# Batch 1 of a Fourier mixing kernel in the form of batches 2 to 7, its additions at written-out times, the extra channel two steps later, and two chunks' last row through TensorE

## The chip, the cores and the metric

The kernel runs on one core of one Trainium2 chip. The metric is the device time of one execution in microseconds (us); the time before is the median of three runs. Engine names in the profile: PE (TensorE, the matrix engine; PEld is its weight loads), DVE (VectorE), ACT (ScalarE), POOL (GpSimd), SP (SyncE, which here only issues DMAs).

## The reference

The input `x` has 8 batches of 3008 rows and 256 channels. Each batch goes through a two-dimensional Fourier transform (over rows and over channels), of which the real part is kept. The result, as 24064 rows of 256, goes through a two-layer network with an ELU between:

```python
X = np.fft.fft(np.fft.fft(x, axis=1), axis=2).real
h = X.reshape(24064, 256) @ w_in                    # w_in: 256 x 2048
g = np.where(h > 0, h, np.exp(np.minimum(h, 0)) - 1)
out = g @ w_out                                     # w_out: 2048 x 256
```

`x` is float32; `w_in` and `w_out` come as 64-bit floats and are converted on the chip.

## The kernel before, in words

**Use of symmetry.** The real part of the transform is a cosine part minus a sine part. Rows k and 3008 - k of the result share both parts with opposite signs, so the kernel computes 1504 columns per batch (one per row pair), 12032 in all, and gets two output rows from each. The channel transform is folded into the first weight matrix: `Wsc` holds the cosine half `Wc` and the sine half `Ws` of the folded `w_in`.

**The main loop.** The columns are cut into 47 tiles of 256, and the 16 blocks of 128 hidden units into 8 pairs. One pair of one tile is a slot; there are 376, some 4.75 us each. A slot does: P, two matmuls of `Wc` with the ring buffer `Rr` into a PSUM bank H (`mm_P`); V, VectorE adding the one extra channel with the weights `wex` (`even_part`, line 1352, writes E); Q, two matmuls of `Ws` with the ring `Ir` into the same bank (`mm_Q`); the minus row from E and H (line 1366); the ELU of both rows (four ACT instructions, two VectorE instructions at line 1382, all into G); four sums on POOL (`sum_1` to `sum_4`); and seven matmuls with `w_out` (`mm_X1` to `mm_X3`, from slot 16 on; eight plain ones, `mm_plain`, before). H has three PSUM banks.

**The transforms.** The rings hold 2048 columns, so a batch's transform must be done shortly before its columns come up: batch 1 begins in tile 5 (slot 40). For each batch there are four: cosine or sine (`ri`) by even or odd output index (`kodd`). Each is made of an even and an odd half, one PSUM bank each, placed between two slots. Two forms exist:

- `Dft` (batches 0 and 1): rows s, 1504 - s and their mirrors are folded first (`mirror_folds` for batch 1, thirty POOL instructions on tiles of 128 x 1536), then three matmuls per half: widths 189, 189 and 378 for the even half and three of 377 for the odd half (or 188, 188, 376 and three of 376). The matrices are `MC`.
- `Quarter` (batches 2 to 7): the rows are folded once more. A batch is loaded in a near and a far set of 96 (or 94) partitions and four rows each (`load_quarter` by indirect DMA on POOL or by SP, `load_odd` by SP), then come `mirror_sum` (POOL), `half_sum` (VectorE), `channel_fold` (POOL), `channel_edge` (ACT), `quarter_pairs` (POOL for even, VectorE for odd index), `turn_pairs` and `shift_pairs` (VectorE). Each half then takes four matmuls, of about 95 columns each (or, for the odd index's odd half, 95 and 94). The matrices are `QM`, 96 rows of them. `unfold`, `finish`, `unfold_odd` and `join` on VectorE put the result into the rings.

**The weights.** `w_in` and `w_out` come in eight chunks each. `Chunk.steps` converts one: exponent and mantissa by integer instructions on VectorE (lines 408 and 420), three ACT steps, then on POOL a rounding sum (line 603, "w<-raw,w"), on VectorE the sign (line 462), on POOL the product and, for `w_in`, two pair sums. The tiles named pow are shared: the next chunk's exponent step waits for the product before. Chunks 5 to 7 of `w_in` and 4 to 7 of `w_out` are converted in slots 7 to 14. `fold_chunk` folds a chunk of `w_in` by TensorE, `put_chunk` copies it to `Wsc` on ACT. The last row of `Ws` must also become two columns of `wex`: for chunks 0 and 1 by `turn_last_row` (two one-column matmuls) and `put_last_row` (ACT), for chunks 2 to 7 by `spread_last_row`, two SP DMAs through DRAM.

**The extra channel.** Channel 128 of all batches is loaded separately (`load_ext`, `get_ext`), folded, transformed by twelve matmuls (`dft_ext`), copied to SBUF (`ext_side`), unfolded and added on VectorE into the tile `rx`, and from DRAM spread over the ring `Rb` (`spread_ext`).

**The order.** Every piece of work is an event with a nominal time: `at(t, fn)`, with 4.8 us per slot (T). The list `FRONT` gives the first 34 us by name, the rest is slot times T plus an offset. Events are sorted and emitted, and `pin` keeps this order on each compute engine; an engine runs its instructions strictly in that order. DMAs issued on SP without `pin` may be placed elsewhere by the scheduler of the framework; on SP too, each waits for the one ahead. Nominal times only order the work; real times are later (slot 12 has nominal 57.6 us and its P begins at 97.55).

Of the kernel before, what the change touches and what calls it, by code (L numbers as in the profile page):

```python
# [9 lines left out]
FP = mybir.dt.float32  # L10
# [167 lines left out]
def kernel(  # L178
# [381 lines left out]
    def load_quarter_mats(ri, kodd):  # L560
        t = cpool.tile([128, BW], FP, tag=f"MC{ri}{kodd}", name=f"QM{ri}{kodd}")
        QM[ri, kodd] = t
        n = sum(QW[i % 2] for i in range(2 * ri + kodd))
        nc.sync.dma_start(
            out=t[0:96, 0 : QW[kodd]], in_=QM_dr.ap()[:, n : n + QW[kodd]]
        )
# [166 lines left out]
    def mirror_folds(L):  # L733

        ops = []
        rows = [t.rearrange("p (m d) -> p m d", d=ND) for t in L]
        for j, k in ((3, 2), (0, 1)):
            own, other = rows[j], rows[k][:, ::-1]
            for m in range(6):
                ops.append(  # L740
                    lambda own=own, other=other, m=m: gtt(
                        own[:, m, 1:], own[:, m, 1:], other[:, m, :0:-1], ALU.add
                    )
                )
            ops.append(
                lambda own=own, other=other: gtt(
                    own[:, :, 0:1], own[:, :, 0:1], other[:, :, 0:1], ALU.add
                )
            )
        EO = [None] * 4  # L750
        for kodd in range(2):
            z = L[1 + kodd]
            for n in range(4):
                c = slice(384 * n, 384 * n + 384)
                ops.append(
                    lambda z=z, c=c, kodd=kodd: gtt(
                        z[:, c], L[0][:, c], L[3][:, c],
                        ALU.subtract if kodd else ALU.add,
                    )
                )  # L760
            for ri in range(2):
                t = EO[2 * ri + kodd] = spool.tile(
                    [128, 768], FP, tag=f"{'eo'[ri]}{1 + 2 * kodd}", bufs=1, name="eo"
                )
                for h in range(2):

                    def fold(z=rows[1 + kodd], t=t, ri=ri, h=h):
                        src = z[:, 3 * h : 3 * h + 3]
                        lo, hi = (
                            v.rearrange("p m (d o) -> p m o d", o=2)  # L770
                            for v in (src[:, :, 1:129], src[:, :, 255:127:-1])
                        )
                        o = t[:, 384 * h : 384 * h + 384]
                        o = o.rearrange("p (m o d) -> p m o d", o=2, d=64)
                        if ri:
                            gtt(o, lo, hi, ALU.subtract)
                        else:
                            gtt(o, lo[:, :, ::-1], hi[:, :, ::-1], ALU.add)

                    ops.append(fold)  # L780
                if not ri:
                    o = t.rearrange("p (m o d) -> p m o d", o=2, d=64)
                    state["edge", kodd] = lambda o=o, z=rows[1 + kodd]: act(
                        o[:, :, 0, 63:64], z[:, :, 0:1]
                    )
        return EO, ops

    def lines(j, far):

        return state["L", j, far].rearrange("p (m d) -> p m d", d=ND)  # L790

    def mirror_sum(j, far, m):

# [6 lines left out]
    def half_sum(kodd, far, h):  # L800
# [3 lines left out]
        for m in (2 * h, 2 * h + 1):  # L804
            vtt(o[:, 3 - m], a[:, m], b[:, m], ALU.subtract if kodd else ALU.add)
# [1321 lines left out]
```

## Time and profile before

| | |
|---|---|
| median of three runs | 1906.9 us (1906.72 to 1908.05) |
| the profiled execution | 1907.61 us |
| its span, first to last instruction | 1905.8 us |
| granted TensorE clock | 1.000 |
| TensorE busy | 1896.7 us |
| VectorE busy | 1488.2 us |
| POOL busy | 1353.5 us |
| ACT busy | 880.2 us |

A line of the timeline gives start, length, engine, line of the kernel, operation, the tiles it writes and reads, how many such instructions follow each other, and in brackets the idle time before it with what ended that. A TensorE matmul in float32 is recorded as two records (so "x4" is two matmuls). Their ends are modelled, so a small gap on PE is better read from the starts: records of 256 columns follow each other every 0.216 us. A line of the groups gives count, total busy time in us, mean in ns, and idle time in front with its releasers.

### The profile page before, as it was taken

The numbers are of one execution on the slowest core, as the hardware profiler recorded it, in microseconds if no ns is written. First come the engines' busy times: TensorE is split into PE (matmuls) and PEld (weight loads), VectorE is DVE, ScalarE is ACT, GpSimd is POOL, SyncE is SP. The second block draws the span as 40 slices with busy tenths as digits, with TensorE's granted clock in tenths as the row PEclk, the third lists the DMA queues.
The fourth block names the chain that finished last, engine by engine and source line by source line (L and its number), as shares of the span: only waits on it lengthen the run. The fifth ranks groups of instructions, "written<-read, shape, count | busy, mean of one in ns | idle before, by whom it ended". The sixth has DMA issues, their size and how long they took to land.

```text
span 1905.8 us, 27983 instructions
## 1 busy us (share of the span) xinstructions
PE 1896.7 (100%) x8972; PEld 1646.7 (86%) x8972; DVE 1488.2 (78%) x2836; ACT 880.2 (46%) x1723; POOL 1353.5 (71%) x1846
## 2 busy tenths in 40 slices
PE   9999999999999999999999999999999999999999
PEld 6888888888888888888888888888888888888887
DVE  8766667888878888778877788877888778777666
ACT  5754444444444444444444444444444444444443
POOL 4887667786677766777667777687766777556664
PEclk9999999999999999999999999999999999999999
DMA  8146211211011110111102111022110210100101
GB/s 340 45 33 44 54 24 45 53 24 36 12 45 41 32 33 12 46 40 30 31 20 49 35 27 30 13 56 44 25 24 16 55 20 15 17 12 15 20 12 23
DMA packets 278934, 73.66 MB, mean 39 GB/s; under 512 B 254402, under 2 KB 268998, under 8 KB 278788
## 3 DMA queue, kind: packets, MB, share of 16 engines
q1 hardware_dynamic: 270148, 61.44, 16.0%
q0 software_dynamic: 6464, 10.18, 1.7%
q8 instruction: 71, 1.16, 0.3%
q14 instruction: 75, 0.61, 0.1%
q10 hardware_dynamic: 2176, 0.26, 0.1%
HBM read 46.96 MB, written 24.80 MB: 38 GB/s over the span
## 4 chain that ended last, share of the span: by engine, by line
PE 96%; DVE 2%; DMA 1%; ACT 1%; issue 0%; POOL 0%; ACTq 0%; POOLq 0%; DVEq 0%
PE H L594 37%; PE pB L594 17%; PE pC L594 17%; PE pD L594 17%; PE pA L594 9%; DMA xl<-in_x_dram,ix 0%; DVE e L691 0%; DVE E L1352 0%; DVE o L691 0%; DVE pow L462 0%; POOL w L603 0%; ACT Wsc L606 0%; ACT G L606 0%; ACT M L606 0%; DMA wex<-wx 0%
## 5 line engine op out<-in xcount | busy, mean ns | idle before, releaser
L603 POOL TENSOR_TENSOR G<-G 128x256 f32<-128x256 f32 x1437 | 1047.4, 738 | 498.6 <-DVE G L1382 343.6
L606 ACT ACTIVATE G<-H 128x512 f32<-128x512 f32 x376 | 224.8, 598 | 917.4 <-DVE G L1366 913.7
L1352 DVE SCALAR_TENSOR_TENSOR E<-Rb,wex,H 128x256 f32<-128x256 f32 x752 | 327.7, 477 | 310.8 <-PE H L594 303.9
L594 PE MATMUL H<-Rr,Wsc 128*128 128x256 f32 x1504 | 388.0, 380 | 0.5 <-ACT Wsc L606 0.5
L594 PE MATMUL H<-Ir,Wsc 128*128 128x256 f32 x1504 | 386.8, 380 | 1.5 <-DVE E L1352 1.5
L594 PE MATMUL pC<-G,WT 128*128 128x256 f32 x1440 | 369.5, 379 | 0.0
L594 PEld LDWEIGHTS H<-Ir,Wsc 128*128 128x128 f32 x1504 | 278.5, 189 | 49.3 <-DVE E L1352 3.9
L594 PEld LDWEIGHTS H<-Rr,Wsc 128*128 128x128 f32 x1504 | 281.6, 190 | 41.6 <-issue 2.3
L594 PEld LDWEIGHTS pC<-G,WT 128*128 128x128 f32 x1440 | 273.6, 190 | 37.2
L1366 DVE SCALAR_TENSOR_TENSOR G<-E,H 128x512 f32<-128x512 f32 x376 | 257.4, 685 | 45.1 <-POOL G L603 11.8
L1382 DVE SCALAR_TENSOR_TENSOR G<-G,H 128x512 f32<-128x512 f32 x376 | 256.4, 682 | 40.0 <-ACT G L606 39.9
L1382 DVE SCALAR_TENSOR_TENSOR G<-M,G 128x512 f32<-128x512 f32 x376 | 257.5, 685 | 0.7 <-ACT M L606 0.7
L606 ACT ACTIVATE G<-G 128x512 f32<-128x512 f32 x376 | 233.4, 621 | 0.0
L594 PE MATMUL pA<-G,w 128*128 128x256 f32 x784 | 229.4, 379 | 0.0
L594 PE MATMUL pB<-G,w 128*128 128x256 f32 x784 | 229.3, 379 | 0.0
L594 PE MATMUL pD<-G,w 128*128 128x256 f32 x784 | 229.3, 379 | 0.0
L606 ACT ACTIVATE M<-G 128x512 f32<-128x512 f32 x376 | 224.1, 596 | 2.8 <-DVE G L1366 1.5
L606 ACT ACTIVATE M<-M 128x512 f32<-128x512 f32 x376 | 221.1, 588 | 0.1
L594 PE MATMUL pB<-G,WT 128*128 128x256 f32 x720 | 214.6, 380 | 0.0
L594 PE MATMUL pD<-G,WT 128*128 128x256 f32 x720 | 214.2, 379 | 0.0
L594 PEld LDWEIGHTS pA<-G,w 128*128 128x128 f32 x784 | 148.9, 190 | 20.7 <-DVE G L1382 0.3
L594 PEld LDWEIGHTS pB<-G,w 128*128 128x128 f32 x784 | 148.9, 190 | 20.4 <-PE H L594 0.2
(171 smaller groups left out, 1584.2 us busy)
## 6 DMA issues: line engine op xcount, KB each, us to landing
out_dram<-ot SPq DMA_DIRECT2D x496, 32.0 KB
xq<-in_x_dram SPq DMA_DIRECT2D x48, 94.0 KB
out_dram<-ot SPq DMA_DIRECT2D x256, 2.0 KB
Rb<-r SPq DMA_DIRECT2D x10, 376.0 KB
raw<-in_moe_w_in_dram SPq DMA_DIRECT2D x7, 512.0 KB
MC<-dft_mats SPq DMA_DIRECT2D x3, 943.5 KB
xq<-in_x_dram SPq DMA_DIRECT2D x12, 192.0 KB
xq<-in_x_dram SPq DMA_DIRECT2D x36, 64.0 KB
```

What stands on the lines that cost most here:

```text
L594: nc.tensor.matmul(out_, lhsT=lhsT, rhs=rhs, start=start, stop=stop, skip_group_check=True)
L603: pin(nc.gpsimd.tensor_tensor(out=o, in0=a, in1=b, op=op))
L606: pin(nc.scalar.activation(out=o, in_=i, func=func, **kw))
L1352: nc.vector.scalar_tensor_tensor(out=S.E[:, c], in0=Rb[:, cols(i)], scalar=wex[:, f : f + 1], in1=S.H[:, c], op0=ALU.mult, op1=ALU.add,)
L1366: nc.vector.scalar_tensor_tensor(out=two(S.G[:, 0:512])[:, :, ::-1], in0=two(S.E), scalar=2.0, in1=two(S.H), op0=ALU.mult, op1=ALU.subtract,)
L1382: nc.vector.scalar_tensor_tensor(out=o, in0=e, scalar=-1.0, in1=h, op0=ALU.add, op1=ALU.max)
```

## The change

Batch 1 is loaded, folded and transformed in the `Quarter` form; `mirror_folds`, `load_x` for batch 1, and the helpers `at_half` and `at_dft` go. In `FRONT`, the four near loads of batch 1 stand at 14.06 (lines 3 and 0 from SP), 15.24 and 16.44 (line 2), 16.44 and 19.2 (line 1); its far loads come at 56.3 to 71.5. All its folding steps stand at times of their own. The four transforms begin at steps 28, 34, 38 and 44 (before: 26, 34, 37, 42).

The four quarter matrices share the two sine `MC` tiles (`MC10`, `MC11`) and are loaded at 34.6 nominal in place of 245 to 288; the turn table moves from step 34 to step 8, the index table (`quarter_table`, four small POOL instructions) from step 27 to 10.0. The extra channel's loads move by 0.8 steps, its transform from step 29 to 31; the copies `ext_side` now stand together in step 32 (before: two in step 30, two in step 33), the odd index's copies lie in free parts of `rx`, and `ext_unfold`, `ext_up` and `ext_down` of the even index stand together in step 32 (before: steps 30, 31 and 32). Chunks 6 and 7 of `w_in` get their last row by `turn_last_row` and `put_last_row`.

```diff
-    def load_quarter_mats(ri, kodd):
-        t = cpool.tile([128, BW], FP, tag=f"MC{ri}{kodd}", name=f"QM{ri}{kodd}")
...
+        home = [
+            cpool.tile([128, BW], FP, tag=f"MC1{i}", name=f"QM{i}") for i in range(2)
+        ]
+        for ri in range(2):
+            for kodd in range(2):
+                w = QW[kodd]
+                c = 0 if ri else QW[1 - kodd]
+                QM[ri, kodd] = t = home[ri == kodd][:, c : c + w]
+                nc.sync.dma_start(out=t[0:96], in_=QM_dr.ap()[:, n : n + w])
+                n += w
...
-    def mirror_folds(L):
...
-    def half_sum(kodd, far, h):
+    def half_sum(kodd, far, h, tt):
...
-            vtt(o[:, 3 - m], a[:, m], b[:, m], ALU.subtract if kodd else ALU.add)
+            tt(o[:, 3 - m], a[:, m], b[:, m], ALU.subtract if kodd else ALU.add)
...
-        t = spool.tile([128, 384], FP, tag="side", bufs=2, name="side")
+        if kodd and rows == NB:
+            t = state["rx"][:, RUN + NO * (1 - par) :]
+        else:
+            t = spool.tile([128, 384], FP, tag="side", bufs=2, name="side")
...
-    names["L"] = lambda: [open_x(1)] + [state["loads"][n]() for n in (4, 5)]
-    for n in range(4):
-        names[f"L{n}"] = lambda n=n: state["loads"][n]()
+    names["L"] = lambda: [
+        fn(1, j, 0) for j in (3, 0) for fn in (load_quarter, load_odd)
+    ]
+    for n, (fn, j) in enumerate(
+        ((load_quarter, 2), (load_odd, 2), (load_quarter, 1), (load_odd, 1))
+    ):
+        names[f"L{n}"] = lambda fn=fn, j=j: fn(1, j, 0)
...
-        (16.44, "w3p u3b Wc2 Xb1 b+3 w3R h3"),
+        (16.44, "w3p u3b Wc2 Xb1 b+3 w3R h3 L1 L2"),
...
-    for c, t in ((2, 15.2435), (3, 23.1265)) + tuple((c, (2 * c - 1) * T + 0.04) for c in range(4, 8)):
+    for c, t in ((2, 15.2435), (3, 23.1265)) + tuple((c, (2 * c - 1) * T + 0.04) for c in (4, 5)):
         at(t, lambda c=c: spread_last_row(c))
+    for c in (6, 7):
+        at((2 * c - 1) * T + 3.02, lambda c=c: turn_last_row(c))
+        at((2 * c - 1) * T + 3.03, lambda c=c: put_last_row(c))
...
-    at(29 * T + 4.75, dft_ext)
-    at(30 * T + 1.46, lambda: ext_side(0))
-    at(30 * T + 1.47, lambda: ext_side(1))
-    at(30 * T + 4.25, lambda: ext_unfold(0, vtt))
-    at(31 * T + 4.25, ext_up)
-    at(32 * T + 4.25, ext_down)
-    at(33 * T + 1.46, lambda: ext_side(2))
-    at(33 * T + 1.47, lambda: ext_side(3))
...
+    at(31 * T + 4.75, dft_ext)
+    at(32 * T + 1.46, lambda: ext_side(0))
+    at(32 * T + 1.47, lambda: ext_side(1))
+    at(32 * T + 1.48, ext_open)
+    for g in (2, 3):
+        at(32 * T + 1.49, lambda g=g: ext_side(g))
+    at(10.0, quarter_table)
+    at(7.2 * T, load_quarter_mats)
...
-    for step, ri, kodd in ((26, 0, 0), (34, 1, 0), (37, 0, 1), (42, 1, 1)):
-        at_dft(step, 2, 1, ri, kodd, lambda k=2 * ri + kodd: state["EO"][k])
...
+    for t, fn, *key in (
+        (23.22, mirror_sum, 3, 0, 1),
+        (26.00, quarter_row, 1),
+        (28.00, mirror_sum, 3, 0, 0),
+        (29.07, mirror_sum, 3, 0, 3),
+        (30.13, mirror_sum, 0, 0, 2),
+        (32.31, mirror_sum, 0, 0, 1),
+        (33.05, mirror_sum, 0, 0, 3),
+        (33.06, mirror_sum, 0, 0, 0),
+        (39.32, mirror_sum, 3, 0, 2),
+        (39.33, half_sum, 1, 0, 0, vtt),
+        (44.10, half_sum, 0, 0, 0, vtt),
+        (44.12, half_sum, 0, 0, 1, vtt),
+        (44.52, channel_fold, 0, 0, 0, 0),
+        (44.52, half_sum, 1, 0, 1, vtt),
+        (45.23, channel_fold, 1, 0, 0, 0),
+        (46.73, channel_fold, 0, 1, 0, 0),
+        (51.51, channel_fold, 1, 0, 0, 1),
+        (52.26, channel_fold, 0, 0, 0, 1),
+        (55.43, channel_edge, 0, 0),
+        (56.33, load_quarter, 1, 0, 1),
+        (56.38, load_odd, 1, 0, 1),
+        (58.91, channel_fold, 1, 1, 0, 0),
...
+        (61.86, channel_fold, 0, 1, 0, 1),
+        (63.71, load_quarter, 1, 3, 1),
...
+        (68.12, channel_fold, 1, 1, 0, 1),
...
+        (76.02, mirror_sum, 0, 1, 0),
...
+        (155.20, ext_unfold, 0, vtt),
+        (156.21, ext_up, 0, vtt),
+        (157.11, ext_down, 0, vtt),
...
+    ):
+        at(t, lambda fn=fn, key=key: fn(*key))
+
+    for step, ri, kodd, finish, join in ((28, 0, 0, 0, 31), (34, 1, 0, 0, 37), (38, 0, 1, 42, 53), (44, 1, 1, 50, 54)):
+        at_quarter(step, 1, ri, kodd, finish, join)
```

## The prediction

> **What bounds the kernel now.** First I read the page's busy times and its chain of work that ended last: is one engine the bound from end to end?
>
> ```profile
> PE 1896.7 (100%) x8972; PEld 1646.7 (86%) x8972; DVE 1488.2 (78%) x2836; ACT 880.2 (46%) x1723; POOL 1353.5 (71%) x1846
> ...
> PE 96%; DVE 2%; DMA 1%; ACT 1%; issue 0%; POOL 0%; ACTq 0%; POOLq 0%; DVEq 0%
> ```
>
> TensorE is on the chain for 96% of the span, so a matmul removed shortens the run unless a new wait appears. The chain in order of time gives the prices. Columns are start, length, what; "PE H x10" is four ordinary H records (0.86) and the six of one half transform of batch 1, "x12" is four and the eight of one half transform of batch 2.
>
> ```profile
> 157.25 0.86 PE H L594 x4
> ...
> 173.22 2.14 PE H L594 x10
> ...
> 184.86 2.77 PE H L594 x10
> ...
> 431.91 1.76 PE H L594 x12
> ```
>
> Third, the waits of PE and its timeline (start, length, idle before it). Records issue every 0.216 us, so eight take 1.73 and a gap is read from start to start. Five gaps behind 30 us matter here: 34.65 (0.77), 59.62 (0.70), 101.02 (98.41 + 1.73 = 100.14, so 0.88), 112.95 (110.62 + 1.73, so 0.60) and 215.36 (0.3).
>
> ```profile
> 59.62 1.13 PE L594 MATMUL H<-Rr,Wsc 128*128 128x256 f32 x4 [0.54 <-ACT Wsc L606]
> ...
> 101.02 1.13 PE L594 MATMUL H<-Ir,Wsc 128*128 128x256 f32 x4 [0.72 <-DVE E L1352]
> ...
> 112.95 1.13 PE L594 MATMUL H<-Ir,Wsc 128*128 128x256 f32 x4 [0.44 <-DVE E L1352]
> ```
> ```profile
> 215.36 1.13 PE L594 MATMUL H<-Ir,Wsc 128*128 128x256 f32 x4 [0.31 <-DVE E L1352]
> ```
>
> VectorE's timeline says what made E late: at 98.88 a chunk's exponent step waited for POOL's product (the shared tile pow), at 112.03 the extra row's weights were still in a DMA.
>
> ```profile
> 98.88 0.43 DVE L408 TENSOR_SCALAR pow<-raw 128x512 int32<-128x512 int32 x1 [2.17 <-POOL w L603]
> ...
> 102.08 2.30 DVE L462 SCALAR_TENSOR_TENSOR pow<-raw,pow 128x512 int32<-128x512 int32 x1
> ...
> 112.03 0.87 DVE L1352 SCALAR_TENSOR_TENSOR E<-Rb,wex,H 128x256 f32<-128x256 f32 x2 [1.92 <-DMA wex<-wx]
> ```
>
> **The change, part by part.** The sum is made on the profiled execution (1907.61 us, span 1905.8) and taken as a difference from the median, 1906.9, which is 0.7 below it.
>
> *Transforms of batch 1 on TensorE.* Eight half transforms go. Their chain pieces are 2.14, 2.77, 2.14, 2.77, 2.13, 2.76, 2.13, 2.76 = 19.60; less 8 x 0.86 of ordinary H work this is 12.72 us. Batch 2's eight pieces are all 1.76: 8 x (1.76 - 0.86) = 7.20. On the path, since PE has no cover: **-5.52 us**. Ends: 7.20 is a like-for-like row, so I give it 0.1 either way. In those pieces a 95-column record takes 0.112 us; a 256-column one, at 0.216, would scale to 0.080. [...]
>
> *Last row of chunks 6 and 7.* Two SP DMAs each go; two one-column matmuls (four records) and a small copy on ACT come. The only clear row is the same step for chunk 1: it starts at 34.65 and the next matmul at 35.12, so 0.47 each: **+0.94**. Chunk 7's DMA was what released E at 112.03, so its 0.60 gap goes: **-0.60**. Chunk 6's DMAs were issued at 94.31 and 95.47 and E of its slot began at 100.10, behind VectorE; nothing is won. The new wait: PE now stands behind ACT's copy of the folded chunk to Wsc. For chunk 6 that copy ends at 94.29 and PE reaches the place at 95.82: covered by 1.5. For chunk 7 it ends at 108.25 and PE arrives at 108.03; queued behind are all later matmuls. Price 0 if the 2.30 us exponent step at 102.08 shortens, 1.0 if that chain slips with the slot 12 delay below; I take **+0.2**, the measured difference.
>
> *The first sums, slots 5 to 14.* POOL had 14 mirror instructions in slots 6 to 9 (twelve of mean 0.94 us) and almost no idle from 71.3 to 94.9. Now seven mirror sums (0.73, in the later batches' rows) stand before slot 7, where POOL was idle 3.56 us, one in slot 8, three folds (0.84 each) in slot 9 and two in slot 10. Its four near indirect DMAs become two, with two more in slots 11.7 and 13.3 (1.2 each); SP's four large loads become sixteen of 0.4 us, in a stretch where SP stands idle till 41.48. VectorE gets the half sums: 2 instructions behind E of slot 8, 6 behind E of slot 9. Nearest row:
>
> ```profile
> L600 DVE TENSOR_TENSOR xq<-xq,xq 96x256 f32<-96x256 f32 x48 | 32.7, 718 | 0.0
> ```
>
> A 256-wide addition with one PSUM operand takes 0.415 (u<-v,pC). Cover: VectorE's idle before E, 1.30 us in slot 8 and 2.89 in slot 9. Two at 0.72 are 1.44, so E of slot 9 moves from 80.02 to about 80.2, still before its matmul at 81.54. Six at 0.42 are 2.5 and fit into 2.89; six at 0.72 are 4.3 and would move E of slot 10 by 1.4, past its margin of 0.66 (start 87.39, latest 88.05): a stall of 0.8. In that stretch POOL waits for ACT until about 84, so I take the lower: 0. [...]
>
> Does the 0.88 gap at 101.02 go? POOL's backlog does, but the chain into it is serial: the minus step of slot 10 ended at 91.0, nine ACT steps ran to 96.12, then two POOL steps of 1.3, then the exponent steps. ACT, later by the half sums, starts that chain at about 91.4. Ends: -0.88 and +0.8; I take **+0.2**.
>
> *Far loads, the weight sums, slots 12 to 17.* POOL gains two DMAs (2.4) and two folds (1.7) against one half sum of 1.0 before the conversion at 112.87, in front of which it sat idle 3.05: covered. Behind it, a fold and a mirror sum (1.6) replace two half sums (2.0) before the first tile sums at 130.16. **0.**
>
> *Slots 17 to 56.* Per batch, VectorE's groups of the later batches add up to some 43 us (half sums 11, turns 15, the rest 17) against 7 for the old form: +36 in 46 slots that have about 1.85 idle each, 85 in all. POOL: 30 against 29. A tile sum may come about 1.5 us late (sum 2 ended at 155.1, its matmul at 156.66). Crowded is slot 32: four side copies on ACT (0.48 each, two before), then three additions for the extra channel (1.22 for the pair, 0.67, 0.61; formerly one slot each): 2.5 us into 1.85, less what waits for ACT anyway. Ends 0 and 0.9; I take **+0.2**. Taking the other two side copies out of slot 33 removes the late G behind the 215.36 gap: **-0.3**. The quarter matrices and turn table load 120 us earlier than needed: 0; the iotas are 0.46 on POOL ahead of a 1.3 us margin: 0.
>
> Sum: -5.52 + 0.94 - 0.60 + 0.2 + 0.2 + 0.2 - 0.3 = **-4.9**: 1906.9 - 4.9 = **1902.0 us** (the profiled execution by itself: 1902.7).
>
> **Rivals.**
> - *The backlog was the cause.* With POOL free the exponent step waits no more: the 0.88 gap, the 0.2 at slot 12 and the 0.2 wait for the chunk copy go. For it: POOL without idle for 23 us. Against it: the serial ACT chain. 1902.0 - 1.3 = 1900.7.
> - *Collisions in the first sums.* Half sums at 0.72, E of slot 10 late (0.8), the copy of chunk 7 late (1.0 in place of 0.2), slot 32 at its upper end (0.9 in place of 0.2). For it: the conversion steps at 0.95 and 1.51 beside 0.42. 1902.0 + 2.3 = 1904.3: within 0.2%.
> - *Slower: batch 1's lines come late.* The first mirror sum now stands in POOL's queue at about 52.5 us, before two weight chunks; POOL waits in order. Slack is the 1.24 idle at 56.42; after that every microsecond of lateness passes to the copy at 58.98 and the matmul at 59.62. It decides from 1.24 + 4.9 = 6.1 us late, and is slower by over 0.2% from 9.9; at 10 late 1910.8. For it: SP's queue is in order, and the wx issue sat until 43.64. Against it: VectorE's last read of those tiles started at 16.9 us, and the loads of before were out by 34.7.
>
> That the form doesn't change is excluded: all four of batch 1's transforms go to the quarter class.
>
> **How the numbers follow.** 0.2% is about what a measurement of this kernel can tell from no change: 3.8 us, so faster means under 1903.1. The likeliest case has 0.58, its own range is 1901.2 to 1903.3 (slot 12, the copy and slot 32 at their nearer ends), and all but 0.06 of it is faster. The backlog rival has 0.14, the collisions 0.19, late lines 0.09. Faster: 0.52 + 0.14 = 0.66; same: 0.06 + 0.19 = 0.25; slower: 0.09. The range runs from 1900.6 (the backlog rival) to 1905.4 (the collision rival, and 1.1 for a slot 12 gap that doubles beside it); outside it lie the late lines and a little of the rest.
>
> **What would show it.** In the chain, batch 1's pieces read about 1.76 with x12 and no x10 is left beyond 170 us. One-column matmuls stand 0.47 apart twice more, and no E waits for wex from 105 on. The PE gap near 101 is still 0.7 to 1.2, near 215 none. VectorE's half sums of slot 9 read about 0.42 each; at 0.7 the collisions hold, and E of slot 10 starts after 88. POOL's first mirror sum starts by 53 with no DMA as its releaser. The prediction is wrong if PE gaps between 50 and 250 us add up to more than 4, or if the 95-column records stand wider than 0.112.

## The result, and the profile after

The changed kernel takes 1912.32 us (median of 8 runs, 1910.78 to 1917.63) where the kernel before takes 1906.9 us (8 runs, 1906.69 to 1908.05): 1.0030 times as long, with a 95% interval of 1.0021 to 1.0039. It is slower by about 5.4 us; the forecast was 1902.0 and faster. Its times also spread wider than before's. The profiled execution is one of the two long ones, 1917.45 us with a span of 1915.7, so the account below is of such a run. One execution each of two later versions, e12 and e13, took 2630 and 2478 us at a granted clock of 0.71 and 0.75; the times below leave them out.

The page of the changed kernel: busy times, and the chain that ended last.

```profile
PE 1895.8 (99%) x8996; PEld 1647.7 (86%) x8996; DVE 1518.6 (79%) x2910; ACT 880.8 (46%) x1731; POOL 1357.7 (71%) x1858
...
PE 88%; DMA 2%; SPq 1%; DVE 1%; POOL 0%; issue 0%; ACTq 0%; ACT 0%; DVEq 0%; POOLq 0%
```

TensorE's share of the chain fell from 96% to 88%, and SP's queue is on the chain for the first time. The work itself became shorter, as forecast; in the chain in order of time the five pieces of batch 1 that stand on it read like batch 2's (two of them here), and the other three take the same 0.86 us from start to start in the timeline:

```profile
230.13 1.76 PE H L600 x12
253.09 1.76 PE H L600 x12
```

What was lost are waits. TensorE's timeline of the changed kernel (start, length, idle before it and what ended that):

```profile
52.73 1.13 PE L600 MATMUL H<-Ir,Wsc 128*128 128x256 f32 x4 [2.62 <-DVE E L1292]
...
92.46 1.13 PE L600 MATMUL H<-Ir,Wsc 128*128 128x256 f32 x4 [0.81 <-DVE E L1292]
...
99.49 1.13 PE L600 MATMUL H<-Ir,Wsc 128*128 128x256 f32 x4 [0.72 <-DVE E L1292]
...
106.56 1.13 PE L600 MATMUL H<-Ir,Wsc 128*128 128x256 f32 x4 [1.17 <-DVE E L1292]
...
208.75 2.07 PE L600 MATMUL H<-Ir,Wsc 128*128 128x256 f32 x4 [6.31 <-DVE E L1292]
...
244.56 0.70 PE L600 MATMUL pB<-G,WT 128*128 128x256 f32 x2 [0.55 <-POOL G L609]
```

Read from start to start, as the prediction did, each gap is some 0.16 longer, and the record behind it starts another 0.10 late (the four records from 52.73 on take 0.97 us, to 53.70, and not 0.86). A gap of 0.73 at 62.20 is the one that the kernel before has at 59.62. The others fall into three places.

**A, 52.73 us.** VectorE's E of the third chunk's slot stood for 2.66 us waiting for the extra row's weights:

```profile
51.80 0.87 DVE L1292 SCALAR_TENSOR_TENSOR E<-Rb,wex,H 128x256 f32<-128x256 f32 x2 [2.66 <-DMA wex<-wx]
```

SP's issue of that DMA in this trace, and in the kernel before with the E that needed it:

```profile
45.83 0.52 SPq L652 DMA_DIRECT2D wex<-wx  x1
```
```profile
45.94 0.39 SPq L646 DMA_DIRECT2D wex<-wx  x1
48.76 0.88 DVE L1352 SCALAR_TENSOR_TENSOR E<-Rb,wex,H 128x256 f32<-128x256 f32 x2 [0.43 <-PE H L594]
```

It was not late but slow: it landed after some 5.9 us, where before it was there by 48.76, in 2.8 at most. Ahead of it in SP's queue now stand batch 1's near loads, ten of them from 31.43 to 40.12 and three more between the two DMAs of the extra row. From its issue to its landing the DMA engines were busy for 0.27 of the time (before: 0.05), so they were not full; how the loads in front would slow it, these traces do not show.

**C, 92 to 107 us.** VectorE's timeline: its half sums in slot 9, and the conversion steps behind them.

```profile
83.75 2.09 DVE L606 TENSOR_TENSOR xq<-xq,xq 96x256 f32<-96x256 f32 x6
...
88.87 1.34 DVE L408 TENSOR_SCALAR pow<-raw 128x512 int32<-128x512 int32 x1
90.14 1.49 DVE L420 TENSOR_SCALAR w<-raw 128x512 int32<-128x512 int32 x1
91.55 0.86 DVE L1292 SCALAR_TENSOR_TENSOR E<-Rb,wex,H 128x256 f32<-128x256 f32 x2
...
93.53 2.44 DVE L462 SCALAR_TENSOR_TENSOR pow<-raw,pow 128x512 int32<-128x512 int32 x1
```

The same places of the slots in the kernel before:

```profile
83.21 0.42 DVE L408 TENSOR_SCALAR pow<-raw 128x512 int32<-128x512 int32 x1
83.55 0.95 DVE L420 TENSOR_SCALAR w<-raw 128x512 int32<-128x512 int32 x1
87.39 0.87 DVE L1352 SCALAR_TENSOR_TENSOR E<-Rb,wex,H 128x256 f32<-128x256 f32 x2 [2.89 <-PE H L594]
...
89.38 1.04 DVE L462 SCALAR_TENSOR_TENSOR pow<-raw,pow 128x512 int32<-128x512 int32 x1
```

The six half sums of slot 9 cost 0.35 us each and the two of slot 8 0.60, both less than forecast. The steps behind them cost more: 1.34, 1.49 and 2.44 us where 0.42, 0.95 and 1.04 stood. E of slot 10 starts at 91.55 with no idle time before it, so TensorE waits for it. The third gap, at 106.56, is the one that the forecast knew at 101.02 (an exponent step that waits for POOL's product); it grew by 0.45.

**D, 200 to 250 us.** ScalarE's and VectorE's timelines around 207 us:

```profile
206.63 0.42 ACT L612 ACTIVATE xq<-xq 1x256 f32<-1x256 f32 x1 [9.85 <-DMA xq<-in_x_dram]
206.96 0.19 ACT L612 ACTIVATE o<-xq 94x4 f32<-94x4 f32 x1
```
```profile
207.18 0.73 DVE L832 SCALAR_TENSOR_TENSOR o<-o,twist_tab,e 94x128 f32<-94x128 f32 x2 [8.70 <-ACT o L612]
```

ScalarE's one-row copy for batch 2 (quarter_row) waited 9.85 us for batch 2's near lines; behind it in ScalarE's order stood batch 1's channel edge, behind that a turn on VectorE, behind that E, behind that TensorE. SP's queue says why these lines were late; first the changed kernel, then the kernel before:

```profile
127.54 2.65 SPq L319 DMA_DIRECT2D xq<-in_x_dram  x6
130.28 8.30 SPq L1133 DMA_DIRECT2D x<-in_x_dram  x4
...
188.12 10.71 SPq L1133 DMA_DIRECT2D x<-in_x_dram  x4
198.92 2.64 SPq L319 DMA_DIRECT2D xq<-in_x_dram  x1
```
```profile
109.81 6.20 SPq L1182 DMA_DIRECT2D x<-in_x_dram  x4
...
164.34 6.67 SPq L1182 DMA_DIRECT2D x<-in_x_dram  x4
```

The extra channel's 16 loads (load_ext: 1,536 single elements each) began 20.5 us later than before, of which some 5 are the delay of everything behind A and C. Batch 1's far loads of line 2 stand ahead of them, and in front of those SP waited 7.6 us for the landing of the second of POOL's far gathers (the changed kernel, POOL's timeline and SP's waits from 112 to 130 us: how much in total, how often, the longest):

```profile
115.55 1.53 POOL L303 DMA_INDIRECT xq<-in_x_dram,ix  x1 [0.18 <-issue]
```
```profile
SPq L336 <- DMA xq<-in_x_dram,ix: 12.3, 2, 7.6
```

That gather landed at 126.78, 11.2 us after its start, and SP's next load went out at 126.79. A POOL fold that the same loads also need, among the weight sums at 122.44, had ended by 123.3. Their last four ended at 198.8 instead of 171.0, and batch 2's first near load followed at 198.92. The consumers had been moved by two slots, some 10 us; the loads moved by 20 to 28.

**The account of this execution**, every gap read from start to start. Transforms -5.5; one-column matmuls of chunks 6 and 7 +0.7, and +0.2 since the record behind each pair is 0.08 late; the two gaps that went, -0.6 and -0.5; A +2.8; C: three gaps of 0.97, 0.88 and 1.33 against one of 0.88, +2.3; D: 6.5 at 208.75, 1.9 for the slow records behind it (last section) and 1.9 in four small waits for POOL, +10.3; the second late record behind each gap, seven against three, +0.4; a front that ended 0.3 earlier, -0.3. Together +9.8; measured, span against span, +9.9.

### The profile page after: what moved, and what is told of

Same layout as the page of the kernel before. It is cut to its first block, busy times and chain, and to the rows that moved or that the text cites. A ratio compares the mean times of both kernels' runs of the same rounds, so it can differ in the third digit from the quotient of the medians.

```text
span 1915.7 us, 28156 instructions
## 1 busy us (share of the span) xinstructions
PE 1895.8 (99%) x8996; PEld 1647.7 (86%) x8996; DVE 1518.6 (79%) x2910; ACT 880.8 (46%) x1731; POOL 1357.7 (71%) x1858
## 3 DMA queue, kind: packets, MB, share of 16 engines
q1 hardware_dynamic: 271638, 62.20, 16.5%
## 4 chain that ended last, share of the span: by engine, by line
PE 88%; DMA 2%; SPq 1%; DVE 1%; POOL 0%; issue 0%; ACTq 0%; ACT 0%; DVEq 0%; POOLq 0%
PE H L600 34%; PE pB L600 16%; PE pC L600 15%; PE pD L600 15%; PE pA L600 8%; DMA x<-in_x_dram 1%; SPq L1527 0%; SPq L1133 0%; POOL G L609 0%; DMA xs<-xe_dr 0%; DVE G L1322 0%; DVE ot L1484 0%; SPq L319 0%; DVE v L606 0%; DVE rx L606 0%
```

## The experiments

Each run was timed against the kernel before on the same chip; the ratio is to those runs.

| run | edit | us | ratio, 95% interval |
|---|---|---|---|
| e1 | changed kernel again, one run | 1909.58 | |
| e2 | chunk 2's last row by TensorE | 1910.78 | 1.0015, 1.0005 to 1.0024 |
| e3 | extra channel's loads earlier | 1922.39 | 1.0083, 1.0066 to 1.0100 |
| e4 | e2 and e3 | 1918.03 | 1.0057, 1.0040 to 1.0073 |
| e5 | before, last row of chunks 6, 7 alone | 1907.40 | 1.0000, 0.9991 to 1.0009 |
| e6 | e2, extra loads made cheap | 1906.06 | 0.9991, 0.9982 to 1.0000 |
| e7 | e2, weight sums spread | 1911.98 | 1.0025, 1.0016 to 1.0034 |
| e8 | e7, near half sums after slot 11 | 1916.74 | 1.0051, 1.0037 to 1.0065 |
| e9 | e2, near half sums in VectorE's idle times | 1909.65 | 1.0014, 1.0006 to 1.0023 |
| e10 | e2, SP's queue reordered | 1910.04 | 1.0016, 1.0007 to 1.0025 |
| e11 | e9 and e10 | 1912.22 | 1.0024, 1.0014 to 1.0034 |
| e12 | e2, POOL's fold first, SP's stores later | 1908.71 | 1.0004, 0.9995 to 1.0014 |
| e13 | e12 and half sums placed again | 1907.56 | 1.0001, 0.9993 to 1.0010 |
| e14 | e13 and three more moves | 1911.76 | 1.0025, 1.0015 to 1.0036 |
| e15 | e14, gathers a slot later | 1908.83 | 1.0004, 0.9995 to 1.0013 |
| e16 | e15, extra loads made cheap | 1906.80 | 0.9998, 0.9989 to 1.0007 |

### A look at the spread (e1)

> The changed kernel as it is, for a second profile. Its profiled execution was among its longest (1917.45 us against a median of 1912.3). Queue theory (the loss is made of transfers that land late: chunk 2's extra-row weights before the gap at 52.73, and batch 2's lines, queued behind the extra channel's loads, before the gap at 208.75): the gap at 52.73 comes back at 2.5 to 3 us, the one at 208.75 (6.3) comes back with another size, and the total moves with it. Collision theory (POOL's folds among VectorE's conversion steps make the loss): the gaps at 92, 99 and 106 (0.97, 0.88, 1.33 from start to start) vary and carry the difference between executions, and the one at 208 does not change.

No edit. The run took 1909.58 us. The gaps at 52 and 93 to 107 us are there again (1.96, 0.80, 0.72 and 1.15 idle), the one near 208 is not, and one of 1.76 at 237 stands in its place. So A and C come in both profiled executions, and D is what differs most between them. A is smaller than the queue theory gave (1.96 idle, 2.12 from start to start, for 2.5 to 3); C did not change, so collisions do not carry the difference between the two.

### Place A (e2)

> The changed kernel with chunk 2's last row also taken by TensorE (two one-column matmuls and an ACT copy) in place of its two DMAs. Queue theory: VectorE no longer waits for the weights at 51.80; it was free at 49.15, in time for TensorE, so the gap of 2.8 us goes against 0.47 for the matmuls: about 2.3 us faster, 1910.0. Collision theory: VectorE's conversion steps before it (1.93 us at 46.28 in place of 0.76) keep E late and at least 1.5 us of the gap stay; gain under 1.

```diff
-        (17.88, "w4b b-3 J-even u1M w4l w3s x-3"),
+        (17.88, "wm2 wex2 w4b b-3 J-even u1M w4l w3s x-3"),
...
-    for c, t in ((2, 15.2435), (3, 23.1265)) + ...
+    for c, t in ((3, 23.1265),) + ...
```

With the last row of this chunk turned by two matmuls (0.37 us) the wait at 52 us is gone. The median falls by 1.5 us (by the ratios to the kernel before, by 2.9) where 2.3 was expected; the executions spread from 1906.61 to 1913.33. A is the wait for that DMA of 128 x 2 single values. That the bulk loads around it slow it is argued from the two queues: no run keeps the DMA and moves the loads. All later experiments but e3 and e5 start from e2.

### The last row on the kernel before (e5)

> The kernel before with one edit of the change alone: the last row of chunks 6 and 7 by two one-column matmuls and a ScalarE copy. Theory (the trace of the changed kernel): 2 x 0.36 us of matmuls on TensorE, against the wait of 0.60 us for chunk 7's last row at 112.95, which goes: +0.1 us, 1907.0, no difference that can be told. The forecast's sum had +0.94 - 0.60 + 0.2 = +0.5: 1907.4. Rival: this edit is a cause of the slower time, by more than 1 us: 1908 or above, with a wait of TensorE for ScalarE or for VectorE's E in slots 11 to 14 that the kernel before does not have.

```diff
-    for c, t in (...) + tuple((c, (2 * c - 1) * T + 0.04) for c in range(4, 8)):
+    for c, t in (...) + tuple((c, (2 * c - 1) * T + 0.04) for c in (4, 5)):
+    for c in (6, 7):
+        at((2 * c - 1) * T + 3.02, lambda c=c: turn_last_row(c))
+        at((2 * c - 1) * T + 3.03, lambda c=c: put_last_row(c))
```

1907.40 beside 1907.68: no difference. This part of the change is no cause.

### Place D: whose loads, and which queue (e3, e4, e6, e7)

> The changed kernel with the extra channel's loads begun 2.9 slots earlier (12.3 in place of 15.2), so that they interleave with batch 1's far loads on SP and do not wait behind the last of them. Queue theory: the last of these loads is issued by about 185 us in place of 199, batch 2's lines land before ACT needs them, the gap near 208 is gone; the median falls by 3 to 4 us to about 1908.8 and the executions lie closer together (they spread over 6.9 us). Collision theory: nothing changes beyond 0.5 us.

```diff
-            (15.2 + 0.5 * n) * T,
+            (12.3 + 0.5 * n) * T,
             lambda j=j, k=k: load_ext(j, 192 * k, 192 * (k + 1)),
```

The opposite of what I expected: 10 us slower than the changed kernel. The stall near 208 did go, but the loads now stood ahead of batch 1's far loads of line 2, which moved from 127.54 to 145.07 us. POOL's mirror sum waited for them, and TensorE for POOL's next G (e3, timelines of POOL and TensorE):

```profile
151.46 0.72 POOL L609 TENSOR_TENSOR xq<-xq,xq 94x255 f32<-94x255 f32 x1 [10.95 <-DMA xq<-in_x_dram]
```
```profile
154.39 1.22 PE L600 MATMUL pB<-G,WT 128*128 128x256 f32 x2 [9.41 <-POOL G L609]
```

Same queue, another victim.

> The two edits together. Queue theory: the gains add, 1912.3 - 2.3 - 3.5 = 1906.5, about the time of before, and what is left of the loss against the forecast of 1902 is in the gaps between 90 and 110 us. Collision theory: 1911 to 1912.

1918.03 us, with a wait of 11.23 for POOL's G at 152.49: e2's and e3's effects stand side by side, and neither expectation held.

> e2 (the changed kernel with chunk 2's last row by TensorE) with the extra channel's 16 loads kept in place, number and order, but each as one contiguous run of 192 elements instead of 192 single elements 1 KB apart. It leaves out the extra channel's right input. Theory (the SP queue: these loads, begun 20 us later than before, hold up batch 2's near lines behind them): the waits of TensorE at about 203 (2.17 us) and 239 (1.61 us) of e2 go, ScalarE's 1x256 copy and POOL's first mirror sum of batch 2 no longer wait for a DMA, and the time falls by 3 to 4.5 us from e2's 1910.78: 1906.3 to 1907.8. Rival (VectorE and POOL simply have too much to do in slots 28 to 33): both waits stay, the time within 0.8 us of e2's.

```diff
-                        offset=x.offset + row * ND + 128,
-                        ap=[[SEQ * ND, NB], [step * ND, s1 - s0], [1, 1]],
+                        offset=x.offset + s0,
+                        ap=[[SEQ * ND, NB], [1, s1 - s0], [1, 1]],
```

The edit leaves out the extra channel's right input. 1906.06 us, 4.7 under e2, and the runs stay within 1905.49 to 1906.94. SP's queue in e2, then in e6:

```profile
127.93 9.15 SPq L1133 DMA_DIRECT2D x<-in_x_dram  x4
...
185.33 7.29 SPq L1133 DMA_DIRECT2D x<-in_x_dram  x4
192.72 3.88 SPq L319 DMA_DIRECT2D xq<-in_x_dram  x1
```
```profile
127.33 1.86 SPq L1133 DMA_DIRECT2D x<-in_x_dram  x4
...
156.84 1.31 SPq L1133 DMA_DIRECT2D x<-in_x_dram  x4
168.14 0.33 SPq L319 DMA_DIRECT2D xq<-in_x_dram  x1
```

The loads begin where e2's begin and are out 34 us sooner; batch 2's lines follow at 168 instead of 193, no wait is left near 203, and of the one of 1.61 near 239 0.47 remains. This settles D, and the spread with it: it is the cost of these 16 loads in a queue that has batch 1's far loads in front and batch 2's lines behind.

> e2 with POOL's weight sums one chunk to a slot (slots 13 to 20) instead of two. Theory: POOL's last fold of batch 1's near lines, which stands among the weight sums at 122.44 us, runs some 5 us earlier, with it SP's six loads of line 2 and, behind them, the extra channel's loads, which begin at about 125 and end by about 190 instead of 199; the waits at 203 and 239 shrink from 3.8 us together to 0.5 to 1.5: 1907.5 to 1908.5. Rival: the loads of the extra channel are paced by the output stores between them in SP's queue, so that they end at the same time and nothing changes: within 0.8 us of e2's 1910.78. A second one: the spread sums stand in front of POOL's G pieces in slots 17 to 20 and TensorE waits there: above 1911.5.

```diff
-        at((12.9 + 0.5 * i) * T + 3.6, lambda i=i: sum_weights(i))
+        at((12.9 + i) * T + 3.6, lambda i=i: sum_weights(i))
```

The second rival held: the wait at 203 went, but not because the loads came sooner. SP's six loads of line 2 went out at 125.52 us where in e2 it is 125.19, since the gather in front of them landed at 124.77, whatever the weight sums did. TensorE itself was later: the spread sums stood ahead of POOL's G pieces, and it waited 0.27, 0.43, 0.43 and 2.53 us from 137 to 156.

### Place C: the half sums (e8, e9)

> e7 with batch 1's near half sums moved from slots 8 and 9, among VectorE's conversions of the weights, to slot 12 and 13, and POOL's folds, the channel edge and the far loads that follow them moved along. Theory (the half sums push VectorE's conversion steps into POOL's steps, where they take 1.2 to 2.4 us instead of 0.4 to 0.7): the waits of TensorE for E at about 91, 98 and 105 of e2 (0.81 + 0.72 + 1.16 = 2.7 us) come back to before's 1.5 or less: 1.0 to 1.5 us under e7. Rival (POOL's own steps of the chunks and not the batch's collide with the conversions, whatever the half sums do): the three waits stay within 0.4 us of e7's, and so does the time.

```diff
-        (39.33, half_sum, 1, 0, 0, vtt),
-        (44.10, half_sum, 0, 0, 0, vtt),
-        (44.12, half_sum, 0, 0, 1, vtt),
-        (44.52, half_sum, 1, 0, 1, vtt),
+        (62.50, half_sum, 1, 0, 0, vtt),
+        (62.51, half_sum, 0, 0, 0, vtt),
+        (65.35, half_sum, 0, 0, 1, vtt),
+        (65.36, half_sum, 1, 0, 1, vtt),
```

The three waits went: the chunk fold of slot 12 starts at 103.78 us, in the kernel before at 103.71, in e2 at 107.48. The time did not come down, since the sums made new waits at their new place, as TensorE's timeline of e8 shows:

```profile
103.78 1.03 PE L600 MATMUL H<-raw,CC 128*128 128x256 f32 x4
...
108.82 1.13 PE L600 MATMUL H<-Ir,Wsc 128*128 128x256 f32 x4 [1.42 <-DVE E L1292]
...
127.72 1.97 PE L600 MATMUL pA<-G,w 128*128 128x256 f32 x8 [2.30 <-DVE G L1322]
```

Next to a busy POOL the four sums took 5.7 us, where in the changed kernel they took 3.3, and ScalarE's edge copies, moved along, waited 3.30 and 3.97 us for POOL's folds with the ELU's copies queued behind them. My reason was half right. Two of the long conversion steps are as long with no half sum near (1.51 and 1.49 at 84 and 85 us), and E of slot 10 still comes in time, since the 2.1 us of half sums ahead of it are gone. Three others became short: the sign steps of 1.39 and 2.44 us took 0.69 and 0.68, a mantissa step of 1.07 took 0.41. POOL's folds of the batch had moved along with the half sums, so e8 shows that batch 1's work in these slots makes E late, and not which share is VectorE's sums and which is POOL's folds beside the conversions.

> e2 with the four near half sums of batch 1 set into VectorE's idle times as the kernel before shows them, ahead of E in slots 8 and 9 (two in slot 9) and ahead of the conversion in slot 11, instead of behind E in slots 8 and 9 (three in slot 9). Theory (the half sums behind E push the conversion steps after them into POOL's steps): the three waits for E in slots 10 to 12, 2.7 us in e2, fall to 1.0 to 1.7, since the conversions keep their place; time 1909.0 to 1909.8, about 1.3 us under e2's 1910.78. Rival (VectorE has no room left in these slots, wherever the sums stand): the sum of the waits from 75 to 110 us stays at 2.5 us or more and the time is e2's.

```diff
+        (39.25, half_sum, 1, 0, 0, vtt),
+        (44.05, half_sum, 0, 0, 0, vtt),
+        (44.06, half_sum, 0, 0, 1, vtt),
+        (51.80, half_sum, 1, 0, 1, vtt),
```

Ahead of E instead of behind it, the waits only changed place: 1.25 us at 78, 1.39 at 99.6 and 0.44 at 106, 3.1 in all against 2.7. Against its own runs of before e9 is where e2 is, 1.0014 and 1.0015: the rival held.

### Reordering SP's queue (e10, e11, e12)

> e2 with two edits of SP's queue: the first four loads of the extra channel ahead of batch 1's far loads of line 2 (where SP stands idle for some 5 us), the other twelve two slots earlier, and each store of a loaded line behind the next two loads instead of straight behind its own (SP stood 8.4 us waiting at the first of these stores). Theory (the end of the extra loads is SP's queue, and they hold up batch 2's near lines): the last extra load is issued by 190 instead of 199, the waits of TensorE at 203 and 239, 3.8 us in e2, fall below 1 us, far loads of line 2 are some 9 us later, POOL's mirror sum waits for them 0 to 3 us and TensorE up to 1 us: 1907 to 1908.5. Rival (the output stores between the loads set their pace, as the spread weight sums left open): the last load as late as before, 1910 to 1911.5. Another (as in e3): TensorE waits over 3 us for POOL's G near 150: 1912 or above.

```diff
-            (15.2 + 0.5 * n) * T,
+            (14.60 + 0.05 * n if n < 4 else 15.2 + 0.5 * (n - 4)) * T,
...
+    for j in range(4):
+        at((15.2 + 0.5 * min(4 * j + 1.1, 11.05)) * T, lambda j=j: store_ext(j))
```

The last extra load was out by 185 us and the wait at 203 went, but line 2's far loads came 8 us later and POOL's mirror sum waited 4.64 us for them, TensorE 3.32 for G at 144: what the second rival says, though at a lower time than it gave.

> e9 and e10 together. Theory: the two causes lie in different stretches (75 to 110 us, and 130 to 250) and add: 1910.78 - 1.3 - 3 = 1905.7 to 1907.2, about the kernel before. Rival: one gives back what the other gains: not under e10.

The rival held: 1912.22, above both, with 4.00 us at 145 and e9's waits.

> e2 with POOL's last fold of batch 1's near lines ahead of the weight sums (at about 115 us instead of 120.66), line 2's far loads behind it as before, the extra channel's first four loads straight behind those, the other loads two slots earlier, and each store behind the next two loads. Theory (the two things that held up SP: the wait for POOL's fold, 7.9 us, and the wait at the first store, 8 us): line 2's loads are issued by 121 instead of 125 to 128, TensorE does not wait for POOL near 144, the last extra load is issued by 190 instead of 199, the waits near 203 and 239 fall from 3.8 to below 1 us: 1907.0 to 1908.3. Rival (the extra loads, packed closer, slow the far loads or the other transfers, and TensorE waits for POOL's G near 144 as in e10): 1909.5 to 1911.

```diff
-        (68.12, channel_fold, 1, 1, 0, 1),
+        (65.30, channel_fold, 1, 1, 0, 1),
```

Together with e10's later stores, and the first four loads straight behind line 2's instead of ahead of them. 1908.71: no wait near 144, but line 2's loads still went out at 125 us, and 1.68 and 1.54 are left at 202 and 237. The fold now ended at 116.2; what SP waited for was the landing of the gather, at 124.31. Between the two expectations.

### Towards a version without the waits (e13 to e16)

> e12 and, of the half sums, two ahead of E in slot 9 (no wait followed in e9), the first behind E in slot 8 (no wait followed in e2) and the fourth ahead of the conversion of slot 12, where VectorE waits 2.5 us for POOL in e2. Theory: the waits for E in slots 8 to 12 fall from 2.7 us to 1.0 to 1.6 and this adds to e12: 1905.5 to 1907.0, at or under the kernel before. Rival (no placing in slots 8 to 12 is free): the waits there stay at 2.5 us or more, and the time at e12's.

```diff
-        (44.10, half_sum, 0, 0, 0, vtt),
-        (44.12, half_sum, 0, 0, 1, vtt),
-        (44.52, half_sum, 1, 0, 1, vtt),
+        (44.05, half_sum, 0, 0, 0, vtt),
+        (44.06, half_sum, 0, 0, 1, vtt),
+        (56.60, half_sum, 1, 0, 1, vtt),
```

1907.56, level with the kernel before. The waits for E in slots 8 to 12 are 1.8 us, a new one of 1.03 stands at 136, and one of 1.59 at 234 that has a plain cause. In e13's SP queue 48 output stores that had piled up behind the extra loads go out in one run, and the odd rows of batch 2's lines, for which POOL waits, stand behind them:

```profile
202.64 23.70 SPq L1529 DMA_DIRECT2D out_dram<-ot  x48
```
```profile
231.31 0.89 POOL L609 TENSOR_TENSOR xq<-xq,xq 96x255 f32<-96x255 f32 x2 [4.55 <-DMA xq<-in_x_dram]
```

> e13 with three more moves: the half sum (0,0,1) from slot 9 to ahead of E in slot 10, where VectorE is idle for 0.97 us in e13; POOL's first far mirror sum of batch 1 behind the last weight sum; and batch 2's near lines 1 and 2 (gather, line 2's last fold before it, and the loads of the odd rows) two to four slots earlier, so that the odd rows are loaded ahead of the 48 output stores behind which they stand in e13 (from 202.64 to 226.34 us). Theory (each wait has its own cause and can be had back): the waits at 83, 136 and 234 fall from 3.6 us together to below 1.2: 1904.3 to 1905.7, faster than the kernel before by about 0.1 per cent. Rival (TensorE's work is not shorter than before's by what the pieces show, or the waits move to POOL's G or to E elsewhere): 1907 to 1908.5 again, with as much waiting in other places.

```diff
+        (48.85, half_sum, 0, 0, 1, vtt),
+        (83.00, mirror_sum, 0, 1, 0),
+        (129.50, channel_fold, 1, 1, 1, 0),
...
+            (0, ((1, 0 if b == 2 else 2, 1.3), (0, 2, 0.2), (3, 3, 0.2), (2, 1 if b == 2 else 3, 1.3))),
```

The wait at 234 went and the one at 83 fell to 0.26; the one at 136 stayed (0.96), and one of 3.71 came at 183: POOL's gather of batch 2's line 1, now earlier, waited for ScalarE's edge copy of batch 1 (e14, POOL's timeline):

```profile
178.65 0.95 POOL L303 DMA_INDIRECT xq<-in_x_dram,ix  x1 [3.23 <-ACT o L616]
```

> e14 with POOL's early gathers for batch 2's lines 1 and 2 one slot later (slots 27 and 28), ScalarE's edge copy of batch 1 before the first of them a little earlier, and POOL's first far mirror sum of batch 1 behind three pieces of G. Theory: the wait of 3.71 us at 183 goes and the one of 0.96 at 136 falls below 0.5, with nothing new above 1 us; the waits for E of 0.26, 0.70 and 0.84 in slots 9 to 12 stay: 1904.5 to 1906.0. Rival (a wait of that size comes up in another place each time, since POOL and SP have no room for the batch two slots later): 1907 or above.

```diff
+            (0, ((1, 1 if b == 2 else 2, 1.3), (0, 2, 0.2), (3, 3, 0.2), (2, 2 if b == 2 else 3, 1.3))),
```

No wait above 1 us is left (0.27, 0.69, 0.85, 0.32, 0.92, 0.15, 0.46), but the time is 1908.83 and not under 1906. In its profile the first matmuls of the front start 2.2 us later than in the kernel before.

> e15 with the extra channel's 16 loads as contiguous runs, as in e6 (it leaves out the extra channel's right input). Theory: of e15's waits those at 138, 187 and 241 (0.32, 0.92, 0.46) go or shrink, those for E in slots 9 to 12 (1.8 together) stay; from the kernel before: transforms -5.5, one-column matmuls of chunks 2, 6 and 7 +1.1, waits +1.8 against before's 1.2 and 0.6, one-column wait gone: 1903.5 to 1905.0. Rival (something else of about 2 us is lost that no wait of TensorE shows): 1905.5 to 1907.

1906.80, the rival's range, again without the extra channel's right input; nearly the same seven waits, 3.6 us in all, and a front that starts like before's. Here the account can be made without a slowed stretch, every gap from start to start: transforms -5.5; one-column matmuls of chunks 2, 6 and 7 +1.1, and +0.2 for the late record behind each; eight gaps of 5.0 in all (one of 0.25 at 97.26 shows no idle time to speak of) against three of 2.0 before, +3.0; the second late record of 0.10 behind each, +0.5; 0.1 at either end, +0.2. Together -0.5; measured, span against span, -0.6. For e6, with five gaps of 4.1, the same sum gives -1.7, and -1.7 was measured. So nothing of note is lost out of sight: small gaps cost more than their idle time says, by 0.16 in the gap itself and 0.10 in the record behind. What the runs settle is where the gain went: the 5.5 us are there in the pieces of the transforms, and batch 1's other work in its new form takes nearly all of them back between 50 and 250 us, in e16 even with the extra loads made cheap. By its median, none of the versions that compute the whole reference beats the kernel before.

## Why the prediction was wrong

- **Transforms, -5.52.** Right: the five pieces of batch 1 on the chain read 1.76 with x12, the other three are as long, no x10 is left.
- **Last row of chunks 6 and 7, +0.94 - 0.60 + 0.2.** Nearly right. The pairs of one-column matmuls cost 0.36 each, not 0.47 (100.46 to 100.82), so +0.7; the gap at 112.95 went; the copy of chunk 7 ended at 112.16, before TensorE came at 113.57, so the +0.2 is 0. The record behind each pair was 0.08 late, +0.2. As a whole: e5, no difference.
- **First sums, "0" for the half sums, +0.2 for slot 12.** The step that failed first. The half sum at 0.42 was near (0.35 in slot 9); what I took from it was wrong. I compared the sums' own length with VectorE's idle time of 1.30 and 2.89 us and let the conversion steps behind them keep their lengths of before. These lengths hung on where POOL was (1.34, 1.49 and 2.44 us where 0.42, 0.95 and 1.04 stood): with its old backlog gone, POOL's chunk steps and the new folds ran beside them. It cost +2.3 from 92 to 107 us: 1.85 in slots 10 and 11, where I had 0, and 0.45 in slot 12, where I had 0.2. "E of slot 10 starts after 88" was my own sign for it, and it started at 91.55; some 2.6 of that is A's delay, and it is still after 88 without them. The rival of collisions had the right place and engine, and priced it at 0.8 in slot 10.
- **SP's loads, costed at nothing.** "Sixteen of 0.4 us, in a stretch where SP stands idle till 41.48" counted the time of issue (and ten of them took 0.87). It didn't ask what stands behind them: a small DMA that someone waits for became slow. A is 2.8 us in the profiled run, 1.5 by e2's median; that these loads are what slowed it is argued, not shown. My rival of late lines had its eye on the same queue and stretch, but on batch 1's lines, which came in time.
- **Far loads, "0"; and slots 17 to 56.** The largest miss. I counted POOL's work there and VectorE's, and for SP only the near loads. For the gathers I counted 1.2 us of POOL each, and not the 9.8 and 11.2 us to their landing, for which SP waits. Batch 1's far loads in SP's in-order queue, this wait in front of them, and the extra channel's loads behind them with batch 2's lines behind those were in no term. It is worth 4.7 us (e6 against e2).
- **215.36, -0.3.** Right that it goes; from start to start, as the other gaps were read, it was 0.47 (the 0.3 is the idle time). **Slot 32, +0.2:** only one small wait stands there, 0.34 us (0.50 from start to start).
- **No rival** had this ending. The sign I named, gaps that add up to more than 4 us between 50 and 250, is what came: 2.8 + 3.2 + 6.5 + 1.9 in the profiled run.

On VectorE beside POOL: the prediction took 0.42 us for a half sum while POOL waits, and kept 0.72 for the collisions. The runs show both sides: six half sums took 0.35 us each with POOL idle (the changed kernel, 83.75 to 85.84), and two took 2.91 us (e13, 98.75 to 101.66) while POOL's product ran beside them from 100.05 to 101.38. Each of the changed kernel's nine TENSOR_SCALAR steps of over 1 us ended 0.3 us after a POOL step (last section).

## What to carry to other kernels

When work is moved between engines, cost every in-order queue that it goes through as a sequence, SP's above all: for each transfer, what it waits for, what stands behind it, and who waits for that; a load that is cheap to issue can wait 7.6 us for a gather to land, and hold up what the critical engine needs some 80 us later. The length of a VectorE step in the trace held only for the POOL step beside it (an exponent step took 0.42 us before and 1.34 in the changed kernel), so moving POOL's work can make VectorE's steps longer. And when each cure moves a stall to another place, as e3, e7, e8, e10 and e14 did, take it as a sign that the engines beside the bound have little room left there; here the gain on the bound had to pay for it.

## What the runs showed of the hardware

**VectorE's long conversion steps ended with POOL's.** Behind the first 30 us of the changed kernel nine TENSOR_SCALAR steps of 128x512 took over 1 us, and each of them ended 0.3 us (0.27 to 0.30) after a POOL instruction: among them those that end at 82.70 (POOL's at 82.43), 90.21 (89.94), 91.63 (91.35) and 97.66 (97.38). The one such step of the kernel before (72.83 to 74.34, POOL's to 74.05) and three of e8 (those at 84.03, 85.46 and 90.89) do so too. With POOL idle such a step took 0.41 us (at 82.63 in the changed kernel). Some of POOL's timeline:

```profile
81.15 1.28 POOL L609 TENSOR_TENSOR w<-w,pow 128x512 f32<-128x512 f32 x1
...
87.77 2.17 POOL L609 TENSOR_TENSOR e<-xq 96x256 f32<-96x256 f32 x2
89.88 1.47 POOL L609 TENSOR_TENSOR w<-w,pow 128x512 f32<-128x512 f32 x1
```

Not every POOL instruction held them up: in the kernel before the step of 0.42 us at 83.21 ran while POOL was in its mirror folds from 82.05 to 85.09. What decides, no run here shows.

**Behind stalls of TensorE of 2.3 us and more its granted clock fell to about a half, but not behind all of them.** Stretches behind a stall (length, busy time and records of PE, PEld, DVE, ACT and POOL, then the granted clock, DMA share and GB/s), first behind the 6.3 us of the changed kernel, then in e2, e7 and e8:

```profile
208.70:212.40 3.70, 3.65 (x9) 2.93 (x10) 3.36 (x12) 0.87 (x3) 0.00 (x0) 0.50 0.83 146
```
```profile
203.80:207.20 3.40, 3.40 (x9) 2.36 (x7) 2.26 (x7) 1.09 (x2) 0.72 (x3) 0.53 0.56 118
```
```profile
156.70:160.00 3.30, 3.30 (x10) 2.58 (x9) 2.34 (x3) 1.62 (x4) 3.12 (x5) 0.51 0.36 60
```
```profile
157.80:161.20 3.40, 3.32 (x15) 2.96 (x16) 1.66 (x2) 0.94 (x2) 3.32 (x6) 1.00 0.36 61
```

In the changed kernel the two groups of four records behind the stall took 1.87 and 1.71 us from start to start instead of 0.86, so the stall cost 1.9 us more than its length. In e2 a gap of 2.33 us from start to start (at 202.75) did the same, some 1.1 us after work had begun again, and cost 1.8; in e7 one of 2.70 (at 155.55) cost 1.7. But one of 2.70 in e8 (at 157.88) and the 2.79 at 52.73 of the changed kernel left the clock at 1.00, so between 2.3 and 2.8 us the length alone did not decide. Behind each of the gaps of 3.0 to 11.4 us in e3, e4, e10, e11 and e14 four records took 1.7 us from start to start.

**Four loads of single elements in a row held SP; one alone did not.** Four loads of 8 x 192 single elements in a row held SP for 8.30 us, four loads of 8 runs of 192 elements for 1.86 (e6). One such load standing alone took 0.35 and 0.32 us of SP (at 155.50 and 162.26 in the changed kernel), as much as one of runs (0.35 and 0.32 in e6).

**A gather landed long after POOL had issued it.** In the changed kernel POOL was busy with one for 0.9 to 1.5 us; it landed 3.4 to 11.2 us after its start, the near ones of batch 1 after 3.9 and 5.9, the far ones after 9.8 and 11.2.
